# Windowed attention and channel mix on one core: every engine in the order of a list schedule, with k and q cast on chip

## The chip, the core and the metric

One NeuronCore of a Trainium2 chip runs the whole program. The metric is the device time of one execution in microseconds. The kernel before took 205.57 us (median of 3 runs, 205.5 to 205.82).

## The reference

Attention with a window of 128 positions and 4 sink positions, over 4 batches, 8 heads, 768 positions, head size 64; then an FFN over the 512 channels of all heads.

```python
scores = scale * q @ k.T                      # scale = 1/8
keep = is_sink | ((rel >= 0) & (rel < 128))   # rel = query position - key position; 4 sinks
a = softmax(where(keep, scores, -1e9))
x = (a @ v), heads side by side               # 4 x 768 x 512
xk = mu_k * x + (1 - mu_k) * x_prev           # x_prev: x of the position before
xr = mu_r * x + (1 - mu_r) * x_prev
out = sigmoid(xr @ w_r) * ((relu(xk @ w_k) ** 2) @ w_v)   # d_ff = 1024
```

## The kernel before

The work is cut into 12 units: `u = 3 b + T` is the 256 positions T of batch b. A unit with T = 0 has no positions before it, needs no sink scores and fewer values; there are 4 such units and 8 others.

**A unit's attention.** `prepare` (L164) transposes k and q on TensorE (L172, four 128x128 transposes a group, four groups a unit) into one bank, and ScalarE copies them out (L175). `sink_scores` (L198) and `scores` (L207) work on pairs of heads (c = 0 to 3): six matmuls (four where T = 0) into the one score tile `sc`, the exponential on ScalarE (L222) into `e`, the mask on VectorE (L228, or L231 where T = 0), then `values` (L234): matmuls of `e` with v (L255) and of the sinks (L244), and on VectorE a reciprocal (L259) and the product (L260) that gives `x`. GpSimd casts v to bf16 (L179).

**A unit's FFN.** `transposed` (L267) turns x (L275, copied by ScalarE at L279), `mix` (L281) makes xk and xr on VectorE (a difference td at L294, four steps each at L298). `ffn` (L302) has the keys (L311: four groups of eight 128x256 matmuls; relu on ScalarE L315, square on VectorE L316), the gate (L323, two groups of four 512-wide matmuls; tanh at L326) and the product (L331, four groups of four 512-wide matmuls; VectorE L336 joins gate and product), and SP stores the result (L339).

**What sets the order.** On TensorE a loop written by hand (L382 to L446): for each n (a unit and a pair of heads) a piece of the current unit's attention, a piece of the FFN of an earlier unit (`fill`), a quarter of the next unit's `prepare`. The order on SP up to unit 2's loads (L86 to L94) is fixed as well; on the other engines a scheduler sets it. Fillers on a tile of zeros (`idle`, L356) stand in TensorE's first part, 35 in all.

**Loads.** For units 0 to 2, k and q come as fp32 through SP's queue and are transposed as fp32. For the others, `load` (L65, L76) issues them from GpSimd's queue with bf16 destinations, so that the transfer casts them. v is always fp32 through SP. Each of k, q and v has three buffers. The weights come as fp32 through SP (L89, L91, L93); w_k and w_r are cast by GpSimd (L366, L369), and w_v is scaled and cast by VectorE (L372).

**PSUM.** Of eight banks two hold `sc`, two are `tps` (transposes, sink scores), one `o`, three `mm`.

Of the kernel before, what the change touches and what calls it, by code (L numbers as in the profile page):

```python
# [13 lines left out]
PSUM = bass.MemoryType.PSUM  # L14


@with_exitstack
def kernel(
# [28 lines left out]
    ld = ctx.enter_context(tc.tile_pool(name="ld", bufs=3))  # L47
    kt_pool = ctx.enter_context(tc.tile_pool(name="kt", bufs=3))
    e_pool = ctx.enter_context(tc.tile_pool(name="e", bufs=3))
    x_pool = ctx.enter_context(tc.tile_pool(name="x", bufs=2))  # L50
    kk_pool = ctx.enter_context(tc.tile_pool(name="kk", bufs=2))
    r_pool = ctx.enter_context(tc.tile_pool(name="r", bufs=3))
# [6 lines left out]
    raw = {}  # L59

    def dtype(u, name):

        return FP32 if u < 3 or name == "v" else BF16

    def load(u, names="kqv", halves=1):  # L65
        b, T = divmod(u, NT)
        for name in names:
            if (u, name) not in raw:
                raw[u, name] = ld.tile([128, 2, H, D], dtype(u, name), name=name + ("s" if dtype(u, name) == FP32 else "b"))
        n = H // halves  # L70
        for i in range(halves):
            for name in names:
                for g in range(2):
                    s0 = 256 * T + 128 * g
                    ahead = dtype(u, name) != FP32
                    ins = (nc.gpsimd if ahead else nc.sync).dma_start(  # L76
                        out=raw[u, name][:, g, n * i:n * i + n, :],
                        in_={"k": k, "q": q, "v": v}[name][
                            b, n * i:n * i + n, s0:s0 + 128, :].rearrange("h p d -> p h d"))
                    if ahead:  # L80
                        tc.keep_in_program_order(ins)

    wk32 = const.tile([128, NC, Dff], FP32, name="wk32")
    wr32 = const.tile([128, NC, Dm], FP32, name="wr32")
    wv32 = const.tile([128, NF, Dm], FP32, name="wv32")
    with tc.manual_schedule(engines={mybir.EngineType.SP}):  # L86
        load(0, "kq", 2)
        load(0, "v")
        nc.sync.dma_start(out=wk32, in_=moe_w_k.rearrange("(c p) f -> p c f", p=128))  # L89
        load(1, "kq")  # L90
        nc.sync.dma_start(out=wr32, in_=moe_w_r.rearrange("(c p) f -> p c f", p=128))  # L91
        load(1, "v")
        nc.sync.dma_start(out=wv32, in_=moe_w_v.rearrange("(c p) f -> p c f", p=128))  # L93
        load(2)  # L94


    warm = const.tile([128, 512], BF16, name="warm")
    nc.vector.memset(warm, 0.0)
    ident32 = const.tile([128, 128], FP32, name="ident32")
    make_identity(nc, ident32)  # L100
    ident = const.tile([128, 128], BF16, name="ident")
    nc.gpsimd.tensor_copy(out=ident, in_=ident32)


    mask = const.tile([128, 2, 2, 2, 128], BF16, name="mask")
    mask0 = const.tile([128, 2, 3, 128], BF16, name="mask0")
# [9 lines left out]
    nc.gpsimd.memset(mask0, 1.0)  # L116
    keep(mask0[:, :, 0, :], "D")
    keep(mask0[:, :, 1, :], "U")
    keep(mask0[:, :, 2, :], "D")
    nc.gpsimd.memset(mask0[0:NS, :, 0:2, :], 1.0)  # L120

    wk_sb = const.tile([128, NC, Dff], BF16, name="wk_sb")
    wr_sb = const.tile([128, NC, Dm], BF16, name="wr_sb")
    wv_h = const.tile([128, NF, Dm], BF16, name="wv_h")
    mu_k_sb = const.tile([128, NC], FP32, name="mu_k_sb")
    nc.scalar.dma_start(out=mu_k_sb, in_=moe_mu_k.rearrange("(c p) -> p c", p=128))
    mu_r_sb = const.tile([128, NC], FP32, name="mu_r_sb")
    nc.scalar.dma_start(out=mu_r_sb, in_=moe_mu_r.rearrange("(c p) -> p c", p=128))

    nc.gpsimd.memset(mask, 1.0)  # L130
    for a in range(2):
        keep(mask[:, a, :, 0, :], "U")
        keep(mask[:, a, :, 1, :], "D")

    v_bufs = [const.tile([128, 2, H, D + 1], BF16, name=f"v{i}") for i in range(3)]
    for t in v_bufs:
        nc.gpsimd.memset(t[:, :, :, D:D + 1], 1.0)

    xts = [const.tile([128, NC, S + 2], BF16, name=f"xt{i}") for i in range(2)]
    for t in xts:  # L140
        nc.gpsimd.memset(t[:, :, 0:2], 0.0)

    ksink = [const.tile([128, NP * 136], BF16, name=f"ksink{i}") for i in range(2)]
    vsink = [const.tile([128, H, D + 1], BF16, name=f"vsink{i}") for i in range(2)]
    for t in ksink + vsink:
        nc.gpsimd.memset(t, 0.0)
    hmask = const.tile([32, H, D + 1], BF16, name="hmask")
    nc.gpsimd.memset(hmask, 1.0)
    nc.gpsimd.affine_select(out=hmask, in_=hmask, compare_op=ALU.is_ge, fill=0.0, base=0,
                            pattern=[[-4, H], [0, D + 1]], channel_multiplier=1)  # L150
    nc.gpsimd.affine_select(out=hmask, in_=hmask, compare_op=ALU.is_ge, fill=0.0, base=3,
                            pattern=[[4, H], [0, D + 1]], channel_multiplier=-1)
    for t in vsink:
        nc.gpsimd.tensor_copy(out=t[0:32, :, D:D + 1], in_=hmask[:, :, D:D + 1])

    spread = const.tile([128, 128], BF16, name="spread")
    nc.gpsimd.memset(spread, 0.0)
    nc.gpsimd.tensor_copy(out=spread[0:NS, 0:4 * H].rearrange("p (h s) -> p h s", s=NS),
                          in_=ident[0:NS, 0:NS].unsqueeze(1).to_broadcast([NS, H, NS]))


    kqt = {}

    def prepare(u, name, half):  # L164
        if half == 0:
            kqt[u, name] = kt_pool.tile([128, NP, 2, 128], BF16, name=name + "t")
        src, dst = raw[u, name], kqt[u, name]
        ps = tr_ps.tile([128, 2, 2, 128], dtype(u, name), name="tps")
        for i in range(2):
            for g in range(2):  # L170
                c = 2 * half + i
                nc.tensor.transpose(out=ps[:, i, g, :],  # L172
                                    in_=src[:, g, 2 * c:2 * c + 2, :].rearrange("p a d -> p (a d)"),
                                    identity=ident32 if dtype(u, name) == FP32 else ident)
        nc.scalar.copy(out=dst[:, 2 * half:2 * half + 2, :, :], in_=ps)  # L175
# [126 lines left out]
    def ffn(u):  # L302
# [25 lines left out]
        for g in range(2):  # L328
            ps = mm_ps.tile([128, Dm], FP32, name="mm")
            for f in range(NF):  # L330
                nc.tensor.matmul(out=ps, lhsT=kk[:, f, 128 * g:128 * g + 128],  # L331
                                 rhs=wv_h[:, f, :], start=(f == 0), stop=(f == NF - 1))
                if f == NF // 2 - 1:
                    yield
# [149 lines left out]
```

## Time and profile before

| what | value |
|---|---|
| median of the runs | 205.57 us |
| the profiled execution | 205.31 us |
| its span | 203.6 us |
| mean granted TensorE clock | 0.966 |
| busy: TensorE, VectorE, ScalarE, GpSimd | 89%, 70%, 61%, 33% |
| transpose of k waiting for its load (kb) | 6.1 us, 4 times, the longest 2.9 |
| GpSimd's DMA issues for k and q | 31.9 us, 36 issues |

The span goes from the first to the last instruction; the profiled execution's own time is 1.71 us longer. Busy shares are of the whole span. L numbers are lines of the kernel before unless the text says otherwise. Names are those of the program (kb, qb: k and q as bf16; kt, qt: transposed; mm: an FFN bank).

### The profile page before, as it was taken

The page shows a single profiled execution, that of the slowest core. Times are in us where ns is not written, and L with a number is a line of the kernel's source. Part 1 is how long each engine was busy: PE and PEld are TensorE (multiplying, and loading weights), DVE is VectorE, ACT ScalarE, POOL GpSimd, SP SyncE. Part 2 cuts the span into 40 slices and gives each one's busy share as a digit, 9 for nine tenths or more (in the row PEclk, how much of TensorE's full clock was granted, in tenths as well). Part 3 has the DMA queues.
Part 4 walks back from the last instruction along what each step waited for, and adds up shares of the span by engine and source line. Part 5 has one row for each costly group of instructions (what it writes and reads, how often), then busy time and mean ns, then how long its engine had stood idle before and what let it go on. Part 6 is the DMA issues. An engine that isn't in the chain of part 4 may idle for free.

```text
span 203.6 us, 4309 instructions
## 1 busy us (share of the span) xinstructions
PE 180.9 (89%) x1681; PEld 115.9 (57%) x1704; DVE 142.5 (70%) x345; ACT 125.2 (61%) x201; POOL 68.0 (33%) x106
## 2 busy tenths in 40 slices
PE   7976869853998999999998999999999999999992
PEld 2633636531584665665855656666647567566650
DVE  0079486950776995986878959858969688698731
ACT  2443527541586586795875785967857868756340
POOL 8947160172149922002389420031890000000000
PEclk9999669996699999999999999999999999999999
DMA  6999999879969999205299992002996011020202
GB/s 117 230 392 212 281 292 279 164 106 166 245 118 127 201 217 67 104 2 131 78 103 181 234 104 106 0 3 106 80 107 125 3 56 48 3 103 3 101 2 103
DMA packets 81572, 25.97 MB, mean 128 GB/s; under 512 B 76432, under 2 KB 76432, under 8 KB 81552
## 3 DMA queue, kind: packets, MB, share of 16 engines
q1 hardware_dynamic: 43056, 20.98, 41.2%
q0 software_dynamic: 37440, 4.72, 36.3%
q8 instruction: 13, 0.21, 0.4%
q10 hardware_dynamic: 1056, 0.00, 0.3%
q14 instruction: 7, 0.06, 0.1%
HBM read 24.12 MB, written 6.29 MB: 149 GB/s over the span
## 4 chain that ended last, share of the span: by engine, by line
PE 37%; DVE 20%; SPq 17%; DMA 10%; ACT 8%; issue 5%; POOL 2%; DVEq 0%; ACTq 0%
SPq L76 13%; PE mm L311 12%; DMA kb<-in_k_dram 8%; PE mm L323 8%; PE mm L331 7%; DVE o_sb L336 5%; DVE xk L298 5%; ACT e L222 4%; ACT kt L175 3%; DVE xr L298 2%; SPq L93 2%; DMA vs<-in_v_dram 2%; PE tps L172 2%; PE o L255 2%; DVE e L228 2%
## 5 line engine op out<-in xcount | busy, mean ns | idle before, releaser
L311 PE MATMUL mm<-xk,wk_sb 128*128 128x256 bf16 x384 | 52.1, 277 | 3.2 <-DVE xk L298 3.1
L222 ACT ACTIVATE e<-sc 128x1024 bf16<-128x1024 f32 (+1 forms) x48 | 45.9, 956 | 10.9 <-PE sc L218 10.1
L331 PE MATMUL mm<-wv_h,kk 128*128 128x512 bf16 x182 | 47.7, 385 | 1.0 <-DVE wv_h L372 0.3
L228 DVE TENSOR_TENSOR e<-e,mask 128x1024 bf16<-128x1024 bf16 x32 | 22.1, 690 | 28.9 <-ACT e L222 28.9
L315 ACT ACTIVATE rl<-mm 128x512 bf16<-128x512 f32 x48 | 28.9, 603 | 20.8 <-PE mm L311 17.6
L311 PEld LDWEIGHTS <-wk_sb 128*128 128x128 bf16 x384 | 35.2, 99 | 10.5 <-issue 5.0
L179 POOL CAST v<-vs 128x512 bf16<-128x512 f32 x24 | 18.5, 788 | 56.4 <-PE o L255 30.8
L298 DVE SCALAR_TENSOR_TENSOR xk<-td,mu_k_sb,xt 128x256 bf16<-128x256 bf16 x48 | 26.1, 578 | 0.0
L331 PEld LDWEIGHTS <-kk 128*128 128x128 bf16 x192 | 16.7, 99 | 14.0 <-issue 1.3
L323 PE MATMUL mm<-wr_sb,xr 128*128 128x512 bf16 x84 | 22.1, 380 | 0.7 <-issue 0.2
L298 DVE SCALAR_TENSOR_TENSOR xr<-td,mu_r_sb,xt 128x256 bf16<-128x256 bf16 x48 | 22.4, 499 | 0.0
L316 DVE TENSOR_TENSOR kk<-rl 128x512 bf16<-128x512 bf16 x48 | 20.0, 417 | 3.1 <-ACT rl L315 3.1
L255 PE MATMUL o<-v,e 128*128 128x65 bf16 x352 | 20.6, 194 | 1.1 <-DVE e L231 1.0
L255 PEld LDWEIGHTS <-e 128*128 128x128 bf16 x352 | 17.7, 98 | 5.9 <-DVE e L231 1.8
L260 DVE TENSOR_TENSOR x<-o,rec 128x256 bf16<-128x256 f32 x48 | 20.1, 420 | 0.7
L231 DVE TENSOR_TENSOR e<-e,mask 128x768 bf16<-128x768 bf16 x16 | 10.3, 641 | 14.8 <-ACT e L222 14.7
L336 DVE SCALAR_TENSOR_TENSOR o_sb<-th,mm 128x512 f32<-128x512 f32 x24 | 16.3, 679 | 4.0 <-PE mm L331 4.0
L175 ACT COPY kt<-tps 128x512 bf16<-128x512 bf16 x18 | 10.5, 583 | 13.9 <-PE tps L172 13.9
L218 PE MATMUL sc<-qt,kt 64*128 64x128 bf16 (+1 forms) x256 | 18.5, 244 | 0.0
L175 ACT COPY qt<-tps 128x512 bf16<-128x512 bf16 x18 | 10.5, 583 | 9.5 <-PE tps L172 9.5
L218 PEld LDWEIGHTS <-kt 64*128 64x128 bf16 x256 | 8.7, 95 | 13.3 <-issue 10.9
L76 POOL DMA_DIRECT2D qb<-in_q_dram x18 | 16.0, 907 | 0.0
(56 smaller groups left out, 211.4 us busy)
## 6 DMA issues: line engine op xcount, KB each, us to landing
vs<-in_v_dram SPq DMA_DIRECT2D x24, 256.0 KB, 5.2
out_dram<-o_sb SPq DMA_DIRECT2D x24, 256.0 KB, 2.0
kb<-in_k_dram POOLq DMA_DIRECT2D x18, 128.0 KB, 5.0
qb<-in_q_dram POOLq DMA_DIRECT2D x18, 128.0 KB, 5.8
wk<-in_moe_w_k_dram SPq DMA_DIRECT2D x1, 2048.0 KB, 9.4
wv<-in_moe_w_v_dram SPq DMA_DIRECT2D x1, 2048.0 KB, 13.6
ks<-in_k_dram SPq DMA_DIRECT2D x4, 256.0 KB, 10.1
qs<-in_q_dram SPq DMA_DIRECT2D x4, 256.0 KB, 5.9
```

Source lines behind the costliest of these rows:

```text
L76: ins = (nc.gpsimd if ahead else nc.sync).dma_start(out=raw[u, name][:, g, n * i:n * i + n, :], in_={"k": k, "q": q, "v": v}[name][b, n * ...
L175: nc.scalar.copy(out=dst[:, 2 * half:2 * half + 2, :, :], in_=ps)
L218: nc.tensor.matmul(out=sc[:, a, o0:o1], lhsT=lhs[rows], rhs=rhs[rows], start=True, stop=True)
L222: nc.scalar.activation(out=e[:, :, lo:], in_=sc[:, :, lo:], func=AF.Exp, scale=scale)
L228: nc.vector.tensor_tensor(out=e, in0=e, in1=mask.rearrange("p a g k q -> p a (g k q)"), op=ALU.mult)
L255: nc.tensor.matmul(out=o[:, g, a, :], lhsT=e[:, a, e0:e0 + 128], rhs=rhs, start=(T == 0 and i == 0), stop=(i == len(blocks) - 1), skip_gro ...
L298: nc.vector.scalar_tensor_tensor(out=dst[:, c0 + i, :], in0=td[:, i, :], scalar=mu[:, c0 + i:c0 + i + 1], in1=prv[:, i, :], op0=ALU.mult, ...
L311: nc.tensor.matmul(out=ps[:, i, :], lhsT=wk_sb[:, c, 128 * f:128 * f + 128], rhs=xk[:, c, :], start=(c == 0), stop=(c == NC - 1), skip_gro ...
L315: nc.scalar.activation(out=rl, in_=ps, func=AF.Relu)
L323: nc.tensor.matmul(out=ps, lhsT=xr[:, c, 128 * g:128 * g + 128], rhs=wr_sb[:, c, :], start=(c == 0), stop=(c == NC - 1))
L331: nc.tensor.matmul(out=ps, lhsT=kk[:, f, 128 * g:128 * g + 128], rhs=wv_h[:, f, :], start=(f == 0), stop=(f == NF - 1))
L336: nc.vector.scalar_tensor_tensor(out=o_sb, in0=th[g], scalar=1.0, in1=ps, op0=ALU.add, op1=ALU.mult)
```

## The change

The loops that emitted the work are replaced. Each step of the work (a group of matmuls, a cast, a load) is now an entry with an engine, a cost in ns, a rank, what it reads and writes, which buffers it takes from a pool and which it holds. `Plan.schedule` simulates the engines with these costs and repeatedly picks the step that can start earliest, with the lower rank first where two could start at the same time. The steps are then emitted in that order under a manual schedule of all engines. Ranks grow by 10 a unit, in the order attention, mix, next unit's preparation, FFN of the unit before.

Beside the order, five things change. All k and q come as fp32 through SP. ScalarE casts each unit's k and VectorE its q, in two halves (512 columns each), so that all transposes are bf16. w_k and w_r are cast by VectorE, no longer by GpSimd. The six PSUM banks beside `sc` are one pool for all uses. Eight fillers remain of 35.

```diff
+FFN_AFTER = 10
+CAST = {"k": "ACT", "q": "DVE"}
...
+                for i in some:
+                    o = ops[i]
+                    t = max(now, at[i])
+                    if o["port"]:
+                        t = max(t, port.get("DVE" if engine == "POOL" else "POOL", 0.0))
...
+                    if pick is None or (t, o["rank"], i) < (pick[0], ops[pick[1]]["rank"], pick[1]):
+                        pick = (t, i)
...
-    sc_ps = ctx.enter_context(tc.tile_pool(name="sc_ps", bufs=1, space=PSUM))
-    tr_ps = ctx.enter_context(tc.tile_pool(name="tr_ps", bufs=2, space=PSUM))
-    o_ps = ctx.enter_context(tc.tile_pool(name="o_ps", bufs=1, space=PSUM))
-    mm_ps = ctx.enter_context(tc.tile_pool(name="mm_ps", bufs=3, space=PSUM))
+    pool("sc", 1, [128, 2, 512], FP32, psum)
+    pool("bank", 6, [128, 512], FP32, psum)
+    for name in ("ks", "qs", "vs"):
+        pool(name, 3, [128, 2, H, D], FP32)
+    pool("kb", 2, [128, 2, H, D], BF16)
+    pool("qb", 2, [128, 2, H, D], BF16)
...
+                P.op("SP", rows * 0.9 + 60.0, emit, rank, service=rows * 1.19 + 60.0,
...
+    for i in range(4):
+        sl = slice(256 * i, 256 * i + 256)
+        P.op("DVE", dve(1024, 0.52), lambda sl=sl: nc.vector.tensor_copy(
+            out=wk_sb[:, :, sl], in_=wk32[:, :, sl]), 2 + i, reads=["wk32"], writes=[("wk", i)],
+            port=True)
...
+            by = CAST[name]
+            if by:
+                copy = {"ACT": nc.scalar.copy, "DVE": nc.vector.tensor_copy,
+                        "POOL": nc.gpsimd.tensor_copy}[by]
+                cost = {"ACT": act(512), "DVE": dve(512, 0.52), "POOL": gps(512)}[by]
+                P.op(by, cost, lambda copy=copy, raw=raw, rk=rk, hs=hs: copy(
+                    out=buf[rk][:, :, hs, :], in_=buf[raw][:, :, hs, :]), rank + half,
...
+    idle(8, -200, ("idle", 0))
+    prepare(0, 0)
+    for u in range(U):
+        attend(u, 10 * u + 4)
+        if u + 1 < U:
+            prepare(u + 1, 10 * u + 11)
+        mix(u, 10 * u + 8)
+        if u > 0:
+            ffn(u - 1, 10 * u + FFN_AFTER)
+    ffn(U - 1, 10 * U + FFN_AFTER)
+    with tc.manual_schedule():
+        P.run()
```

Three places show how the instructions move.

VectorE, unit 0's attention, before (rec and x normalize a pair of heads, td and xk are the mix; the last masks stand between them):

```order
L231 TENSOR_TENSOR e<-e,mask_138 128x2x384
L259 RECIPROCAL rec<-o 128x4
L260 TENSOR_TENSOR x<-o,rec 128x2x128
L231 TENSOR_TENSOR e<-e,mask_138 128x2x384
L192 TENSOR_TENSOR vsink_168<-tps,hmask 32x8x64
L294 TENSOR_TENSOR td<-xt_162 128x512
L259 RECIPROCAL rec<-o 128x4
L298 SCALAR_TENSOR_TENSOR xk<-td,mu_k_sb,xt_162 128x256 x2
L260 TENSOR_TENSOR x<-o,rec 128x2x128
```

And now (wk_119 is the loaded w_k, e_88 and e_89 the last two pairs of heads, bank_62 to bank_64 the values of the first three):

```order
L493 TENSOR_TENSOR e_88<-e_88,mask_128 128x2x384
L493 TENSOR_TENSOR e_89<-e_89,mask_128 128x2x384
L436 TENSOR_TENSOR vsink_133<-bank_67,hmask 32x8x64
L354 CAST wk_sb<-wk_119 128x4x256 x4
L530 RECIPROCAL rec_92<-bank_62 128x4
L530 RECIPROCAL rec_93<-bank_63 128x4
L530 RECIPROCAL rec_94<-bank_64 128x4
L533 TENSOR_TENSOR x_95<-bank_62,rec_92 128x2x128
L533 TENSOR_TENSOR x_95<-bank_63,rec_93 128x2x128
```

The four casts of w_k, which GpSimd had, now stand ahead of all normalization of unit 0.

ScalarE, whose copies follow TensorE's groups, around the first keys of unit 1's FFN (rl), before (the first COPY of kt is unit 3's k, the es and the first e belong to unit 2):

```order
L205 ACTIVATE es<-tps 128x256
L222 ACTIVATE e<-sc 128x1024
L175 COPY kt<-tps 128x512
L222 ACTIVATE e<-sc 128x1024
L279 COPY xt_162<-tps 128x2x256
L175 COPY qt<-tps 128x512
L222 ACTIVATE e<-sc 128x1024
L315 ACTIVATE rl<-mm 128x512 x2
L175 COPY kt<-tps 128x512
```

And now (kt_83 and qt_84 are unit 2's, rl_107 is of unit 1's first keys, kb_78<-ks_68 is the cast of unit 3's k):

```order
L406 COPY kt_83<-bank_63 128x512
L562 COPY xt_129<-bank_65 128x2x256
L406 COPY qt_84<-bank_62 128x512
L484 ACTIVATE e_86<-sc_61 128x1024
L406 COPY qt_84<-bank_63 128x512
L607 ACTIVATE rl_107<-bank_67 128x512
L484 ACTIVATE e_87<-sc_61 128x1024
L457 ACTIVATE es_91<-bank_62 128x256
L382 CAST kb_78<-ks_68 128x2x256
```

The first keys of unit 1 stood behind unit 3's first transposed k and three exponentials of unit 2; now they stand behind one exponential of unit 2 and ahead of all of unit 3.

The loads of unit 3, before on GpSimd (v_157 is unit 1's v, v_158 unit 2's, v_156 unit 3's; kb and qb are unit 3's k and q):

```order
L179 CAST v_157<-vs 128x8x64 x2
L179 CAST v_158<-vs 128x8x64 x2
L76 DMA kb<-in_k_dram 128x8x64 x2
L76 DMA qb<-in_q_dram 128x8x64 x2
L179 CAST v_156<-vs 128x8x64 x2
```

And now on SP (wv_121 is the loaded w_v, ks_70, qs_73 and vs_76 are unit 2's, ks_68, qs_71 and vs_74 unit 3's):

```order
L248 DMA wv_121<-in_moe_w_v_dram 128x8x512
L237 DMA ks_70<-in_k_dram 128x8x64 x2
L237 DMA qs_73<-in_q_dram 128x8x64 x2
L237 DMA vs_76<-in_v_dram 128x8x64 x2
L237 DMA ks_68<-in_k_dram 128x8x64 x2
L237 DMA qs_71<-in_q_dram 128x8x64 x2
L237 DMA vs_74<-in_v_dram 128x8x64 x2
```

Unit 3's k and q stood behind GpSimd's cast of unit 2's v; now they stand directly behind the load of that v.

More of the change, by code (lines that the diff above doesn't have):

```diff
@@ L54, with pool @@
[L54 to L65 removed]
+    psum = ctx.enter_context(tc.tile_pool(name="psum", bufs=1, space=PSUM))
+    P = Plan()
+    def pool(name, n, shape, dtype, where=const):
+        P.pool(name, [where.tile(shape, dtype, name=f"{name}{i}") for i in range(n)])
@@ L71, in load @@
[L71 to L94, printed above, removed]
@@ new lines, with const_op @@
+    for u in range(2, U):
+        load(u, "kqv", -92 if u == 2 else 10 * u - 18)
+    for i, src in enumerate((moe_mu_k, moe_mu_r)):
+        P.op("ACT", 600.0, lambda i=i, src=src: nc.scalar.dma_start(
+            out=mu[i], in_=src.rearrange("(c p) -> p c", p=128)), -100, writes=[("mu", i)],
+            service=300.0)
+    def const_op(engine, cost, emit, writes=(), reads=(), rank=-50):
+        P.op(engine, cost, emit, rank, writes=writes, reads=reads, port=engine == "POOL")
+    warm = tile1([128, 512], BF16, "warm")
@@ L126 @@
[L126 to L159, printed above, removed]
@@ L162 @@
[L162 to L175, printed above, removed]
```

718 lines of the change are left out of this document (460 added, 258 removed).

## The prediction

> **What bounds the kernel now.** I read the page first, then the windows, the chain of waits and TensorE's timeline. The span, TensorE's busy time and the chain's shares by line:
>
> ```profile
> span 203.6 us, 4309 instructions
> ...
> PE 180.9 (89%) x1681; PEld 115.9 (57%) x1704; DVE 142.5 (70%) x345; ACT 125.2 (61%) x201; POOL 68.0 (33%) x106
> ...
> SPq L76 13%; PE mm L311 12%; DMA kb<-in_k_dram 8%; PE mm L323 8%; PE mm L331 7%; DVE o_sb L336 5%; DVE xk L298 5%; ACT e L222 4%; ACT kt L175 3%; DVE xr L298 2%; SPq L93 2%; DMA vs<-in_v_dram 2%; PE tps L172 2%; PE o L255 2%; DVE e L228 2%
> ```
>
> TensorE looks full, but 21% of the chain is the loads of L76 on SP and the k loads (kb). So there are two regimes. In the middle, a window of 60 us from steady running (columns: TensorE, weight loads, VectorE, ScalarE, GpSimd, granted clock, DMA share):
>
> ```profile
> 80.00:140.00 60.00, 58.06 (x606) 38.67 (x613) 48.38 (x123) 43.91 (x72) 17.23 (x22) 1.00 0.66 94
> ```
>
> TensorE is 97% busy at full clock, VectorE 81%, ScalarE 73%. At the beginning it is otherwise. The chain of waits in order of time (start, length, what):
>
> ```profile
> 35.74 4.55 DMA vs<-in_v_dram
> 40.34 0.85 POOL v L179
> 41.19 0.95 POOL kb L76
> 42.14 7.34 DMA kb<-in_k_dram
> 49.53 0.50 PE tps L172 x3
> ```
>
> Unit 3's k is loaded through GpSimd's queue, behind GpSimd's cast of unit 2's v; that v came at 40.3 us. TensorE, whose order puts unit 3's first transposes ahead of the rest of unit 2, then waits until 49.5. The two marks from which I work are the start of unit 1's and of unit 11's FFN in TensorE's timeline:
>
> ```profile
> 54.35 0.39 PE L311 MATMUL mm<-xk,wk_sb 128*128 128x256 bf16 x2
> ...
> 190.86 3.66 PE L311 MATMUL mm<-xk,wk_sb 128*128 128x256 bf16 x32
> ```
>
> Between them lie ten steps of (190.86 - 54.35) / 10 = 13.65 us, and behind the second mark 203.6 - 190.86 = 12.74 us. The execution took 205.31 us, 1.71 over its span, and is 0.26 under the median of 205.57. Before = 54.35 + 10 x 13.65 + 12.74 + 1.71 + 0.26 = 205.57; I predict each term.
>
> **How much of a step is TensorE's own work.** Its timeline in a dense stretch; I read distances from start to start, since the lengths overlap:
>
> ```profile
> 118.87 0.35 PE L255 MATMUL o<-v,e 128*128 128x65 bf16 x6
> 119.05 1.03 PE L331 MATMUL mm<-wv_h,kk 128*128 128x512 bf16 x4
> 119.91 0.39 PE L172 MATMUL tps<-ident,kb 128*128 128x128 bf16 x4
> 120.23 0.39 PE L218 MATMUL sc<-qt,kt 64*128 64x256 bf16 x6
> 120.56 0.40 PE L275 MATMUL tps<-ident,x 128*128 128x128 bf16 x4
> 120.79 1.03 PE L331 MATMUL mm<-wv_h,kk 128*128 128x512 bf16 x4
> ...
> 122.88 0.39 PE L172 MATMUL tps<-ident,qb 128*128 128x128 bf16 x4
> 123.10 1.03 PE L331 MATMUL mm<-wv_h,kk 128*128 128x512 bf16 x4
> ...
> 128.63 0.22 PE L244 MATMUL o<-vsink,es 128*128 128x130 bf16 x1
> ...
> 128.99 1.04 PE L311 MATMUL mm<-xk,wk_sb 128*128 128x256 bf16 x8
> 129.86 0.39 PE L172 MATMUL tps<-ident,qb 128*128 128x128 bf16 x4
> ```
>
> Four 512-wide matmuls take 0.86 us, eight 256-wide 0.87, a group of k transposes 0.32 and of q 0.22, six scores 0.33, x transposes 0.23, one pair of heads through the values 0.36 (0.18 where there is no sink). A unit with sinks is therefore 2 x 0.32 + 2 x 0.22 (k and q) + 0.44 (sink scores, half of eight 256-wide) + 4 x 0.33 + 4 x 0.36 + 2 x 0.23 + 4 x 0.87 (keys) + 2 x 0.86 (gate) + 4 x 0.86 (product) = 13.4 us; a unit that starts a sequence has no sink scores and cheaper values, 12.2. The attentions within the ten steps are seven of the first and three of the second kind: 130.4 us, or 13.04 a step. So only 0.6 of the 13.65 us can be won in a step, while the first mark at 54.35 has much room.
>
> **The change at the first mark.** Up to unit 2 the loads on SP stand in the same order, so weights and v land when they did. Rows of before, from the timeline and from the page's list of DMA issues:
>
> ```profile
> 16.32 4.75 POOL L366 CAST wk_sb<-wk 128x1024 bf16<-128x1024 f32 x4 [3.90 <-DMA wk<-in_moe_w_k_dram]
> ...
> 17.85 2.32 DVE L298 SCALAR_TENSOR_TENSOR xk<-td,mu_k_sb,xt 128x256 bf16<-128x256 bf16 x2
> ...
> 20.09 4.70 SPq L93 DMA_DIRECT2D wv<-in_moe_w_v_dram  x1
> ```
>
> ```profile
> wv<-in_moe_w_v_dram SPq DMA_DIRECT2D x1, 2048.0 KB, 13.6
> ```
>
> w_k is there at 16.3 and w_v at 20.1 + 13.6 = 33.7. The weight casts go from GpSimd to VectorE; the nearest row is VectorE's scaling of w_v, 0.62 for each of four, and two other VectorE rows price what follows (the second gives shortest, median and longest):
>
> ```profile
> 35.78 2.49 DVE L372 TENSOR_SCALAR wv_h<-wv 128x1024 bf16<-128x1024 f32 x4
> ```
>
> ```profile
> L260 DVE TENSOR_TENSOR x<-o,rec 128x256 bf16<-128x256 f32 x48 | 20.1, 420 | 0.7
> ```
>
> ```profile
> L298 DVE SCALAR_TENSOR_TENSOR xk<-td,mu_k_sb,xt x48: 469/477/2110, 17.9 to 190.4; 128x256 bf16<-128x256 bf16 x48
> ```
>
> The four w_k casts stand ahead of unit 0's normalization on VectorE. This is an added wait: queued behind it are the reciprocals and x of unit 0, and TensorE, ScalarE and VectorE wait for these in turn. 16.3 + 4 x 0.62 = 18.8; four x with their reciprocals, at most 0.6 each, 21.2; transposes and copy about 1.0; two td, a q cast and four xk about 3, so unit 0's keys begin near 25. Before, they stand at 24.9 with a stall to 27.6, so this wait replaces one of its size and I give it nothing. Up to 35 TensorE then has keys (3.5), gate (1.7) and unit 1's attention (3.7), 8.9 us: it must wait for w_v. At 33.7 VectorE casts two quarters (35.0) and TensorE begins unit 0's product. All four are done at 36.2, the rest of unit 1's x at 38.0, transposes and copy at 39.0, then td, one q cast, td and four xk, 2.6: unit 1's keys start at **41.6** in place of 54.35. Nothing of unit 3 stands ahead of them, and its loads follow v of unit 2 directly on SP. The earliest is 39 (VectorE hides the x work); the latest 46, if unit 2's k and q come 4 us after w_v, as they are on SP.
>
> Filler matmuls go from 35 to 8. Their cover was the clock. After the wait that ended at 49.5 the window shows it:
>
> ```profile
> 49.00:56.00 7.00, 6.16 (x49) 3.77 (x50) 3.58 (x8) 3.53 (x5) 1.23 (x2) 0.62 1.47 222
> ```
>
> 0.62 over 7 us is 2.7 us lost. The same at unit 0's keys would turn 8.9 us of work into 11.6 from 25 on, 36.6. That is 1.6 us past 35.0, but VectorE is then still casting w_v, to 36.2, and its x work sets the mark; I take 0 and keep 0 to 1.6. The Trainium skill, "TensorE: Matmul & The Clock Gate", Part 1, speaks against dropping fillers: after about 3.4 us of idleness the array runs at half clock until about 3.4 us of sustained work have passed. By it the loss would be an estimated 1.7 us, which leaves the sum as it is; this trace's loss is larger, 2.7, and the measurement decides.
>
> **The change in a step.** GpSimd loses 36 DMA issues; k and q come as fp32 through SP, between its v loads and its stores. From the list of waits:
>
> ```profile
> SPq L339 <- DVE rec L259: 73.8, 10, 11.6
> ```
>
> SP spends 73.8 us waiting in stores, so 36 more issues cost nothing there; a load behind a store could come late, but the loads stand two units ahead. Added are two k casts on ScalarE and two q casts on VectorE a unit. No row shows them; the nearest for ScalarE:
>
> ```profile
> L175 ACT CAST kt<-tps x6: 581/585/586, 6.6 to 40.7; 128x512 bf16<-128x512 f32 x6
> ```
>
> So 1.17 us a step on ScalarE (10.0 + 1.2 of 13.65). On VectorE half of a 0.62 us cast is 0.31, and an isolated one costs at most the 0.42 of L260's row: 0.6 to 0.8 on 11.0. Both stay under TensorE's 13.04. What can go is the rest of 0.6 a step. The fp32 transposes of units 0 to 2 lie before the first mark and are hidden behind loads. From both ends, 13.04 (nothing waits) and 13.9 (0.25 worse for fuller engines), I take **13.4**, nearer the middle since each TensorE group now stands where its operands are planned ready. The slow xk of 17.85 us, 2.32 for two, ran while GpSimd cast w_k; with GpSimd's casts of weights and its issues gone, VectorE's xk should stay at its median 0.48. The Trainium skill, "SBUF — State Buffer", section "SBUF: two separate sides", calls the port pair of VectorE and GpSimd a lock on which the loser blocks wholly. By it the 24 q casts also hold back GpSimd's v casts; the row above agrees with blocking, and an estimated step would lie between 13.04 and 13.4.
>
> Sum: 41.6 + 134.0 + 12.74 + 1.71 + 0.26 = **190.3 us**.
>
> **The rivals.**
> VectorE paces the step, still faster: it is fullest (11.0 + 0.8 of 13.65), and six banks now serve transposes, values and FFN alike, so a late VectorE holds TensorE. Against it: 11.8 is still only 88% of a 13.4 us step. At 14.3 a step the time is 199.3. Chance 0.12.
> The early stall survives in another form: cold clock to the first mark, or unit 2's k and q late, with 50 to 54 there: 198.7 to 202.7. Against it: the loads are no later than before. Chance 0.05.
> Slower than before: VectorE keeps all its present idleness, 13.65 - 11.0 = 2.65 us a step, because its static order meets the exponentials too early, and adds the casts. That is 14.5, or 201.3. It decides from a step of 14.93, where it loses 3.1 us to waits; at 15.2 the time is 208.3. For it: one score tile in both kernels, four masks a unit. Against it: FFN work stands between the masks. Chance 0.07.
> That the change does nothing is excluded by the order, where casts and loads have moved.
>
> **How the numbers follow.** The forecast has 0.76, its own range 186 (39 and 13.2) to 199 (46 and 13.8). The faster rivals fill 199 to 203, where most of VectorE's lies at the lower end. From 185 to 200 holds eight in ten. About 0.2% is what a measurement of this kernel can tell from no change. Faster: 0.76 + 0.12 + 0.04 = 0.92; same 0.01; slower 0.07.
>
> **What would show it.** Right: unit 1's keys near 41.6 us in TensorE's timeline, no wait for kb of several us, ten steps of about 13.4, w_v's casts just before unit 0's product, VectorE under 90% in the middle. Wrong: the first mark past 47; a step over 13.9 with TensorE waiting for VectorE or ScalarE; or low clock after 30 us.

## The result

The changed kernel takes **191.27 us** (median of 4 runs, 190.66 to 192.09) where the kernel before takes 205.69 on the same chip: a ratio of 0.929, 95% interval 0.924 to 0.934. The forecast was 190.3, within 185 to 200. Some executions of any of these kernels are slow ones; ratios and intervals use the fast ones alone, medians all.

The profiled execution took 191.44 us, 13.87 less than the one before. Its page, in the order of the lines shown of before:

```profile
span 189.7 us, 4373 instructions
...
PE 171.4 (90%) x1676; PEld 111.1 (59%) x1676; DVE 155.9 (82%) x375; ACT 133.4 (70%) x225; POOL 31.9 (17%) x65
...
PE bank L598 18%; PE bank L636 18%; PE bank L621 8%; PE sc L476 6%; DMA ks<-in_k_dram 5%; PE bank L517 4%; DVE xk L577 4%; PE bank L395 4%; SPq L237 3%; DVE kk L611 3%; DVE e L493 3%; DVE xr L577 2%; DVE qb L382 2%; PE bank L449 2%; PE bank L556 2%
```

The 21% of the chain that were loads (L76, k, q and v on SP, and kb) are 8% now (ks and L237), and FFN matmuls (L598 keys, L636 product, L621 gate) stand in their place. TensorE's busy time fell by 9.5 us (180.9 to 171.4), its idle time by 4.4 (22.7 to 18.3). The idle time of before is overstated: 23 of its matmuls have no record (1681 against 1704 weight loads), and some of what shows as idle is theirs.

The two marks in TensorE's timeline, the start of unit 1's and of unit 11's keys:

```profile
41.67 0.81 PE L598 MATMUL bank<-xk,wk_sb 128*128 128x256 bf16 x4
...
177.18 3.66 PE L598 MATMUL bank<-xk,wk_sb 128*128 128x256 bf16 x32
```

So the sum is 41.67 + 10 x 13.55 + 12.52 + 1.74 = 191.4. Of the 13.87 us gained, 12.7 lie ahead of the first mark, 1.0 in the ten steps, 0.2 behind. What TensorE did up to that mark, before (windows, then its filler group) and after:

```profile
0.00:54.35 54.35, 41.03 (x303) 24.22 (x306) 28.94 (x56) 23.92 (x37) 26.93 (x53) 0.87 1.08 224
```

```profile
L360 PE MATMUL mm<-warm 128*128 128x512 bf16 x35 | 11.1, 453 | 1.3 <-DVE warm L98 1.3
```

```profile
0.00:41.67 41.67, 29.22 (x239) 17.53 (x239) 27.92 (x60) 23.62 (x37) 16.04 (x41) 0.75 1.04 252
```

```profile
L660 PE MATMUL bank<-warm 128*128 128x512 bf16 x8 | 3.6, 631 | 1.3 <-DVE warm L272 1.3
```

Fillers stand where TensorE would wait. Idle time and fillers together were 54.35 - 41.03 + 11.1 = 24.4 us and are 41.67 - 29.22 + 3.6 = 16.1, so by this count 8.3 of the 12.7 us are waiting that went; 7.5 of these are fillers. The other 4.4 are work that is shorter (bf16 in place of fp32 transposes) or no longer stands ahead of that mark. This split hangs on the clock, 0.87 before and 0.75 here: work at a lower clock takes longer and fills waits. With 27 fillers put back (the last experiment) the clock up to the mark is 0.92 and the mark 41.32. Idle time and fillers are then 41.32 - 32.22 + 10.6 = 19.7 us, and of the 13.0 us by which that mark moved only 4.7 are waiting that went:

```profile
0.00:41.32 41.32, 32.22 (x266) 17.99 (x267) 26.65 (x60) 23.69 (x37) 16.06 (x41) 0.92 1.02 250
```

```profile
L371 PE MATMUL bank<-warm 128*128 128x512 bf16 x21 | 5.4, 379 | 0.0
L666 PE MATMUL bank<-warm 128*128 128x512 bf16 x8 | 3.4, 606 | 1.3 <-DVE warm L272 1.3
...
L371 PE MATMUL sc<-warm 128*128 128x512 bf16 x6 | 1.8, 377 | 2.0 <-ACT e L490 2.0
```

The middle, in the columns of before's row (TensorE, weight loads, VectorE, ScalarE, GpSimd, clock, DMA share, GB/s):

```profile
80.00:140.00 60.00, 58.37 (x596) 37.67 (x594) 55.21 (x134) 46.31 (x79) 9.30 (x14) 1.00 0.63 149
```

TensorE is as full as before (58.37 against 58.06), VectorE is at 92% in place of 81%. All of TensorE's waits after 60 us:

```profile
PE bank L517 <- DVE e L493: 1.5, 2, 1.2
```

### The profile page after: what moved, and what is told of

Same layout as the page of the kernel before. It is cut to its first block, busy times and chain, and to the rows that moved or that the text cites. A ratio compares the mean times of both kernels' runs of the same rounds, so it can differ in the third digit from the quotient of the medians.

```text
span 189.7 us, 4373 instructions
## 1 busy us (share of the span) xinstructions
PE 171.4 (90%) x1676; PEld 111.1 (59%) x1676; DVE 155.9 (82%) x375; ACT 133.4 (70%) x225; POOL 31.9 (17%) x65
## 4 chain that ended last, share of the span: by engine, by line
PE 64%; DVE 20%; DMA 5%; ACT 4%; SPq 4%; issue 2%; ACTq 0%; DVEq 0%
PE bank L598 18%; PE bank L636 18%; PE bank L621 8%; PE sc L476 6%; DMA ks<-in_k_dram 5%; PE bank L517 4%; DVE xk L577 4%; PE bank L395 4%; SPq L237 3%; DVE kk L611 3%; DVE e L493 3%; DVE xr L577 2%; DVE qb L382 2%; PE bank L449 2%; PE bank L556 2%
## 5 line engine op out<-in xcount | busy, mean ns | idle before, releaser
L598 PE MATMUL bank<-xk,wk_sb 128*128 128x256 bf16 x384 | 54.7, 279 | 0.1
L636 PE MATMUL bank<-wv_h,kk 128*128 128x512 bf16 x192 | 47.1, 380 | 0.0
L598 PEld LDWEIGHTS <-wk_sb 128*128 128x128 bf16 x384 | 35.2, 100 | 7.0 <-issue 1.1
L493 DVE TENSOR_TENSOR e<-e,mask 128x1024 bf16<-128x1024 bf16 (+1 forms) x48 | 31.1, 653 | 8.5 <-ACT e L484 8.4
L607 ACT ACTIVATE rl<-bank 128x512 bf16<-128x512 f32 x48 | 29.2, 630 | 7.4 <-PE bank L598 6.6
L413 POOL CAST vb<-vs 128x512 bf16<-128x512 f32 x24 | 17.4, 741 | 74.4 <-DMA vs<-in_v_dram 45.7
L636 PEld LDWEIGHTS <-kk 128*128 128x128 bf16 x192 | 17.1, 98 | 19.1 <-issue 1.1
L621 PE MATMUL bank<-wr_sb,xr 128*128 128x512 bf16 x96 | 24.5, 380 | 0.0
L577 DVE SCALAR_TENSOR_TENSOR xk<-td,mu,xt 128x256 bf16<-128x256 bf16 x48 | 23.2, 507 | 0.5
L577 DVE SCALAR_TENSOR_TENSOR xr<-td,mu,xt 128x256 bf16<-128x256 bf16 x48 | 22.4, 490 | 0.0
L645 DVE SCALAR_TENSOR_TENSOR ob<-th,bank 128x512 f32<-128x512 f32 x24 | 16.3, 681 | 6.7 <-PE bank L636 6.7
L517 PE MATMUL bank<-vb,e 128*128 128x65 bf16 x352 | 20.1, 197 | 1.6 <-DVE e L493 1.5
L533 DVE TENSOR_TENSOR x<-bank,rec 128x256 bf16<-128x256 f32 x48 | 19.6, 419 | 0.7
## 6 DMA issues: line engine op xcount, KB each, us to landing
wv<-in_moe_w_v_dram SPq DMA_DIRECT2D x1, 2048.0 KB, 13.8
```

Source lines behind the costliest of these rows:

```text
L493: nc.vector.tensor_tensor(out=buf[ek][:, :, lo:], in0=buf[ek][:, :, lo:], in1=m, op=ALU.mult)
L517: nc.tensor.matmul(out=o[:, g, a, :], lhsT=e[:, a, e0:e0 + 128], rhs=rhs, start=(T == 0 and i == 0), stop=(i == len(blocks) - 1), skip_gro ...
L533: P.op("DVE", dve(256), lambda ok=ok, rk=rk, c=c: nc.vector.tensor_tensor(out=buf["x", u][:, :, 128 * c:128 * c + 128].rearrange("p g (a d ...
L577: nc.vector.scalar_tensor_tensor(out=buf[key][:, c0 + i, :], in0=buf[tk][:, i, :], scalar=mu[w][:, c0 + i:c0 + i + 1], in1=xt[:, c0 + i, t ...
L598: nc.tensor.matmul(out=ps[:, i, :], lhsT=wk_sb[:, c, 128 * f:128 * f + 128], rhs=xk[:, c, :], start=(c == 0), stop=(c == NC - 1), skip_gro ...
L607: P.op("ACT", act(512), lambda psk=psk, rk=rk: nc.scalar.activation(out=buf[rk], in_=buf[psk].rearrange("p (i t) -> p i t", i=2), func=AF. ...
```

## The experiments

Each was timed against the kernel before on its own chip. Before's median was between 204.91 and 205.53 there, so ratios are compared. Marks and steps are those of each profiled execution.

| kernel | median, us | ratio to before, interval | first mark | step |
|---|---|---|---|---|
| before | 205.57 | 1 | 54.35 | 13.65 |
| before, unit 3's k and q by SP | 204.28 | 0.997, 0.992 to 1.002 | 52.16 | 13.78 |
| changed, second measurement | 191.64 | 0.929, 0.924 to 0.934 | 39.99 | 13.56 |
| changed, casting loads from 12 us on | 200.99 | 0.984, 0.977 to 0.991 | 49.68 | 13.77 |
| changed, casting loads behind unit 2's v | 190.90 | 0.926, 0.921 to 0.930 | 42.65 | 13.46 |
| changed, no casts, fp32 transposes | 196.93 | 0.961, 0.955 to 0.967 | 42.52 | 13.88 |
| changed, order undone at one place | 194.19 | 0.942, 0.938 to 0.946 | 50.81 | 12.94 |
| changed, plan with half costs | 215.73 | 1.048, 1.043 to 1.053 | 47.02 | 15.52 |
| changed, q cast by GpSimd | 190.07 | 0.929, 0.922 to 0.936 | 41.03 | 13.39 |
| changed, q cast by ScalarE | 191.01 | 0.932, 0.928 to 0.937 | 43.15 | 13.39 |
| changed, w_v cast by GpSimd | 194.92 | 0.953, 0.949 to 0.957 | 43.35 | 13.75 |
| changed, q and w_v cast by GpSimd | 200.87 | 0.981, 0.975 to 0.987 | 48.67 | 13.79 |
| changed, fillers kept | 191.87 | 0.941, 0.935 to 0.946 | 41.32 | 13.59 |

The changed kernel measured again sets the scale: its first mark was 41.67 in one profiled execution and 39.99 in the other, and its runs went from 189.88 to 192.55. Less than 1% between two versions is not told apart here.

> The changed kernel itself, so that variants are compared on one chip: 190.5 to 192.2 by every theory.

### Is it unit 3's load alone?

The kernel before, with unit 3's k and q loaded as fp32 through SP, so that they no longer stand behind GpSimd's cast of unit 2's v:

```diff
-        return FP32 if u < 3 or name == "v" else BF16
+        return FP32 if u < 4 or name == "v" else BF16
```

> The kernel before with one line changed: k and q of unit 3 too come as fp32 through SP and are transposed as fp32. Theory A, the early gain is the load of unit 3 that no longer stands behind GpSimd's cast of unit 2's v: the wait of 5.4 us before 49.5 and the 2.7 us of low clock behind it go, unit 1's keys start near 46.3 in place of 54.35, and the time is about 197.5 (196 to 199). Theory B, the early gain is the order, with unit 1's keys ahead of unit 3: the wait only changes its releaser, unit 1's keys stay past 50, and the time is 202 to 205.6.

The time is the same (interval 0.992 to 1.002). TensorE's timeline before, unit 3's first transposes, then that of this kernel with unit 1's keys:

```profile
46.78 0.23 PE L172 MATMUL tps<-ident,kb 128*128 128x128 bf16 x1 [2.89 <-DMA kb<-in_k_dram]
49.53 0.50 PE L172 MATMUL tps<-ident,kb 128*128 128x128 bf16 x3 [2.52 <-DMA kb<-in_k_dram]
```

```profile
46.30 0.30 PE L172 MATMUL tps<-ident,ks 128*128 128x128 f32 x1 [1.94 <-DMA ks<-in_k_dram]
47.40 0.55 PE L172 MATMUL tps<-ident,ks 128*128 128x128 f32 x3 [0.80 <-DMA ks<-in_k_dram]
...
52.16 0.50 PE L311 MATMUL mm<-xk,wk_sb 128*128 128x256 bf16 x3
```

The rest of unit 3's k comes 2.1 us sooner (47.40 for 49.53), and TensorE's two waits for it are 2.7 us in place of 5.4. Mark and time are those of theory B, but theory A had taken the wait as gone, and it is only halved: TensorE's order by hand still stands at it while the FFN of unit 1 is held behind. Halving the wait that the chain named gives 2.2 us at the mark and nothing at the end that can be told. What removing it whole would give no run shows.

### Are the SP loads and the casts what gains?

The changed kernel with k and q of units 3 to 11 loaded by GpSimd with the cast in the transfer, as before, and no casts on ScalarE and VectorE for them. First with nothing to hold these loads back, then with each of them reading the cast of unit 2's v:

```diff
+                    P.op("POOL", 950.0, lambda key=(name + "b", u), src=src, g=g, s0=s0:
+                         nc.gpsimd.dma_start(
+                             out=buf[key][:, g, :, :],
...
+                         reads=[("vb", 2, 1)], writes=[(name, u, g, hp) for hp in range(2)])
...
-            if by:
+            if u > 2:
+                raw = rk
+            elif by:
```

(The first of the two is without the `reads` entry. The second also emits these loads later, each unit's just ahead of its `prepare`.)

> The changed kernel with the load path undone: k and q of units 3 to 11 come as bf16 by casting DMAs on GpSimd's queue, so 36 DMA issues return there and 36 casts leave ScalarE and VectorE; the schedule places them anew. If the load path and the casts make the gain, unit 1's keys start past 46 and the time is 196 or more. If the order makes it, unit 1's keys start at 41 to 44 and, with 0.7 us a unit less on VectorE, the time is 187 to 192.

> The changed kernel with the load path undone as before: k and q of units 3 to 11 by casting DMAs on GpSimd's queue, those of unit 3 only behind the cast of unit 2's v, as in the kernel before; the order around unit 1's keys stays that of the changed kernel. If the order makes the early gain, unit 1's keys start at 41 to 42.5 although unit 3's k comes at 49 or so, and with 24 casts less on VectorE the time is 188 to 191. If the load path is needed for it, unit 1's keys start past 46 and the time is 196 or more.

The first comes out as expected of a gain by the load path (mark 49.68, 200.99 us), the second as expected of one by the order (42.65, 190.90 us). Held back, the old loads are as fast as the new ones with their casts: 0.926 against 0.929, intervals that overlap. From unit 3 on the casts on chip and the loads through SP give nothing by themselves. Let go at once, the twelve loads run beside the weights. GpSimd's timeline of that kernel shows the first of them, SP's the issue of w_v, VectorE's the casts that follow its landing:

```profile
12.74 2.05 POOL L240 DMA_DIRECT2D kl<-in_k_dram  x2
```

```profile
25.63 3.69 SPq L260 DMA_DIRECT2D wv<-in_moe_w_v_dram  x1
```

```profile
41.80 2.50 DVE L375 TENSOR_SCALAR wv_h<-wv 128x1024 bf16<-128x1024 f32 x4 [3.46 <-DMA wv<-in_moe_w_v_dram]
```

In the changed kernel w_v is issued at 20.11 and its casts start at 34.22. So w_v comes 7.6 us later here, of which 5.5 are SP's queue, held up ahead of it, and the rest a slower transfer, and most of the 10 us that this kernel loses is lost there. That the loads keep behind the weights is thus a condition of the gain, though not its source.

The other way about, no casts at all and every transpose of k and q in fp32:

```diff
-CAST = {"k": "ACT", "q": "DVE"}
+CAST = {"k": None, "q": None}
```

> The changed kernel without the casts of k and q: all transposes of k and q are fp32, in a list schedule of their own. In the kernel before, an fp32 group of four transposes is 0.60 long and a bf16 group 0.39, and their spacing 0.58 against 0.22 to 0.32: some 0.3 us more for each of four groups a unit. Theory, TensorE's own work sets the step once VectorE and ScalarE have room: 13.04 + 1.2 = 14.2 to 14.6 a step, and 198 to 202 us. Rival, TensorE's work is covered by waits for VectorE: VectorE loses 1.1 us a unit and ScalarE 1.3, their waits go, and the step stays at 13.5 to 13.9: 191 to 195 us.

196.93 us, 3.9% below the kernel before, though that one has bf16 transposes from unit 3 on and this one has none. The middle, and the spacing of such a group (0.44 from its start to the next, 0.32 and 0.22 for bf16 groups):

```profile
80.00:140.00 60.00, 60.00 (x585) 40.44 (x584) 49.96 (x118) 43.96 (x71) 8.29 (x14) 1.00 0.63 145
```

```profile
88.00 0.60 PE L395 MATMUL bank<-ident,ks 128*128 128x128 f32 x4
88.44 0.22 PE L505 MATMUL bank<-vsink,es 128*128 128x130 bf16 x1
```

TensorE has no idle time left. By this spacing a unit's own work would be 13.04 + 4 x 0.44 - 1.08 = 13.72, and a step takes 13.88. The time lies between the two expectations and the step within the rival's; yet TensorE's own work sets it, as the theory had it, with a surcharge of 0.17 a group in place of 0.3 (before, too, an fp32 group was 0.44 from the next, 38.76 to 39.20; the expectation's 0.58 was too long). So the change gains 3.9% even with transposes that are dearer than before's; the 3% between this kernel and the changed one are about what bf16 transposes are worth, which from unit 3 on the kernel before had too.

### Is it the order?

In the changed kernel, unit 1's second x transposes made to wait for unit 3's first transposed k, as in the order by hand, with unit 3 prepared a unit sooner:

```diff
-                 reads=["ident", ("x", u, c0), ("x", u, c0 + 1)], writes=[psk])
+                 reads=["ident", ("x", u, c0), ("x", u, c0 + 1)] +
+                 ([("kt", 3, 0)] if (u, half) == (1, 1) else []), writes=[psk])
...
-        if u + 1 < U:
-            prepare(u + 1, 10 * u + 11)
+        for w in {1: (2, 3), 2: ()}.get(u, (u + 1,)):
+            if w < U:
+                prepare(w, 10 * w + 1)
```

> The changed kernel with one added dependence: the second x transposes of unit 1 wait for unit 3's first transposed k, as they stood behind it in the kernel before; the schedule places the rest anew, loads and casts stay. If this order is what cost the time before, these transposes start near 46.5 in place of 38.3, unit 1's keys near 50 in place of 41.7, and the time is 197 to 202. If the order there is worth nothing, the time stays within 1 us of the changed kernel's.

The rows of its two marks:

```profile
50.81 2.50 PE L599 MATMUL bank<-xk,wk_sb 128*128 128x256 bf16 x20
...
180.18 3.66 PE L599 MATMUL bank<-xk,wk_sb 128*128 128x256 bf16 x32
```

The mark is 9.1 us later, the profiled execution only 3.0 (194.46), and the step falls to 12.94: 6 us of the later mark are work of units 2 and 3 that TensorE did meanwhile and need not do later. The first mark is where the order would put it (near 50), but the time, 194.19, lies below the 197 to 202 that were expected with it. One place of the order costs 1.4% (0.942 against 0.929), and a mark is not yet a loss.

Then the same list schedule with costs that are wrong:

```diff
+        if engine in ("DVE", "ACT"):
+            cost = 0.5 * cost
```

> The changed kernel with the plan's costs of VectorE's and ScalarE's steps halved, so that the order is made for engines twice as fast. If the early gain needs only an order that keeps later units out of the way, unit 1's keys still start at 41 to 43, the step grows from 13.55 to 13.7 to 14.2, and the time is 193 to 198. If the gain needs the measured costs, the time is 200 or more; if the costs do not matter, it is within 1 us of the changed kernel's.

It is 4.8% slower than the kernel before the change: the gain needs the measured costs. Its middle and its largest waits of TensorE after 60 us:

```profile
80.00:140.00 60.00, 52.42 (x536) 34.99 (x543) 49.00 (x122) 43.86 (x75) 6.38 (x10) 1.00 0.57 129
```

```profile
PE bank L558 <- DVE x L535: 5.6, 7, 1.5
PE bank L519 <- DVE e L495: 5.5, 11, 1.3
PE sc L478 <- ACT e L486: 2.0, 4, 0.8
```

No engine is fuller than in the changed kernel; all are emptier. The same instructions on the same engines, put where VectorE and ScalarE should have been done but are not, give a step of 15.52. That is the mechanism of the prediction's slower rival, and the costs in the plan are what kept it away.

What the change brought beside the order can be bounded at the first mark. Unit 0's product, the first work that needs w_v, starts at 36.52 before and at 34.94 now:

```profile
36.52 1.20 PE L331 MATMUL mm<-wv_h,kk 128*128 128x512 bf16 x4 [0.31 <-DVE wv_h L372]
```

```profile
34.94 2.05 PE L636 MATMUL bank<-wv_h,kk 128*128 128x512 bf16 x8
```

So what acts ahead of it, w_k and w_r cast by VectorE among it, is worth some 1.6 of the 12.7 us there; 11.1 lie behind it, where the order differs. (Unit 2's fp32 transposes stand there too, before; but the kernel without casts has fp32 transposes as well, and its mark is at 42.52.) The six PSUM banks as one pool no run changes alone, so their share stays open.

### What holds a step at 13.55?

The casts of q on GpSimd, and on ScalarE:

```diff
-CAST = {"k": "ACT", "q": "DVE"}
+CAST = {"k": "ACT", "q": "POOL"}
```

> The changed kernel with the q casts on GpSimd. If VectorE, 92% busy in the middle, sets the 0.5 us that a step has over TensorE's own 13.04, the step falls from 13.55 to 13.2 or 13.3 and the time to 187.5 to 189. If GpSimd's casts hold up VectorE as much as they relieve it, or TensorE's own work is all, the time stays within 190.5 to 193.

> The changed kernel with the casts of q on ScalarE as well as those of k. If VectorE's fullness (55.21 of 60 us) is what keeps a step at 13.55 over TensorE's own 13.04, VectorE falls by two casts a unit and the step falls to about 13.4, as it did with these casts on GpSimd: 190 us. Rival: the step is held by the exchange between TensorE and the two engines whichever of them is fuller; ScalarE goes from 46.3 to about 52 of 60 us (two casts of 0.667 a unit) and the step stays at 13.5 to 13.9: 191 to 195 us.

Both have a step of 13.39. The middle with GpSimd's casts, then with ScalarE's:

```profile
80.00:140.00 60.00, 59.73 (x623) 38.60 (x621) 53.59 (x124) 46.57 (x81) 14.29 (x22) 1.00 0.61 145
```

```profile
80.00:140.00 60.00, 59.02 (x606) 37.42 (x600) 52.94 (x126) 52.27 (x92) 8.02 (x13) 1.00 0.65 150
```

With VectorE at 53.6 or 52.9 in place of 55.2, 0.16 us a step go, whichever engine takes the casts. For GpSimd step and time lie between the two expectations; for ScalarE the step is that of the theory and the time that of the rival. On ScalarE the gain is given back at the first mark (43.15): there w_v's casts start at 35.18, 1.0 later than in the changed kernel, and TensorE waits for them:

```profile
35.93 2.06 PE L636 MATMUL bank<-wv_h,kk 128*128 128x512 bf16 x8 [1.10 <-DVE wv_h L363]
```

Neither median can be told from the changed kernel's.

The 0.16 is not yet the price of the casts on VectorE, since each kernel has a list schedule of its own. The middle with w_v's cast on GpSimd, with both w_v's and q's there (next section), and with the casting loads behind v:

```profile
80.00:140.00 60.00, 59.08 (x605) 38.52 (x603) 54.99 (x135) 48.64 (x85) 7.94 (x14) 1.00 0.63 148
```

```profile
80.00:140.00 60.00, 58.89 (x635) 39.70 (x635) 52.27 (x123) 47.70 (x83) 11.52 (x19) 1.00 0.61 144
```

```profile
80.00:140.00 60.00, 58.29 (x597) 37.59 (x603) 55.02 (x129) 43.57 (x72) 20.15 (x28) 1.00 0.82 103
```

Between the first two the q casts leave VectorE and the step goes from 13.75 to 13.79; in the third VectorE has no q casts from unit 3 on, is as full as ever, and the step is 13.46. So that VectorE's fullness holds the step at 13.55 is not shown.

### What sets the first mark?

The scaling and cast of w_v on GpSimd:

```diff
-        P.op("DVE", dve(1024, 0.52), lambda i=i: nc.vector.tensor_scalar(
+        P.op("POOL", gps(1024), lambda i=i: nc.gpsimd.tensor_scalar(
```

> The changed kernel with the scaling and cast of w_v on GpSimd in place of VectorE. Theory C, VectorE's chain sets the start of unit 1's keys: the four casts, 2.47 us at 34.22, stand ahead of the rest of unit 1's x, so without them the keys start up to 2.4 us sooner, 39.3 in place of 41.67, and the time falls by 1.0 to 2.4 us, to 189 to 190.3. Rival: TensorE's own work sets it, since TensorE is busy 11.03 of the 12 us up to the mark; then at most 0.97 us can go and the product of unit 0 waits for GpSimd, which needs about 1.5 us for each of four casts by its v casts (0.741 for half as many columns): the time stays at 191 to 192.5.

GpSimd's row, and TensorE's products that wait for it:

```profile
34.42 11.17 POOL L363 TENSOR_SCALAR wv_h<-wv 128x1024 bf16<-128x1024 f32 x4 [6.51 <-DMA wv<-in_moe_w_v_dram]
```

```profile
37.25 1.01 PE L636 MATMUL bank<-wv_h,kk 128*128 128x512 bf16 x2 [1.92 <-POOL wv_h L363]
...
39.99 1.01 PE L636 MATMUL bank<-wv_h,kk 128*128 128x512 bf16 x2 [1.73 <-POOL wv_h L363]
```

2.8 us a cast, where 1.5 was expected: the product of unit 0, which stands ahead of unit 1's keys on TensorE, became the later path, the mark went to 43.35 and the time past both expectations. So VectorE's chain was not tested by itself. In the changed kernel TensorE has 0.97 us idle in the 12 us up to its mark, and the last xk of unit 1 ends near 42.2 on VectorE; the two paths end within half a microsecond of each other, and which one is last the runs leave open.

Both moves together, q and w_v on GpSimd:

> The changed kernel with the casts of q and of w_v both on GpSimd. If both relieve VectorE where it is the last to come, the gains add: first mark 39 to 40, step 13.4, 188 to 189.5 us. If either place is set by TensorE, the time is within 1 us of the changed kernel's, 190.3 to 192.

200.87 us, later than either and past both expectations: its w_v casts take 11.28 us, and unit 0's last products wait 2.43 for them. The gains expected at two places of the order did not add.

What moves the mark between executions is when w_v's casts start. In the second execution of the changed kernel:

```profile
32.51 2.50 DVE L363 TENSOR_SCALAR wv_h<-wv 128x1024 bf16<-128x1024 f32 x4 [0.25 <-DMA wv<-in_moe_w_v_dram]
```

```profile
39.99 0.75 PE L598 MATMUL bank<-xk,wk_sb 128*128 128x256 bf16 x4
```

The casts start at 32.51 there and at 34.22 in the first, 33.87 with the fillers of the next section, 35.17 with the casting loads behind v; the mark comes 7.48, 7.45, 7.45 and 7.48 us later. So from the start of these casts to the mark the chain has one length in all four, and the 1.7 us between the changed kernel's two marks lie ahead of it.

### Fillers

Twenty-seven fillers put back into the gaps of the first 20 us:

```diff
+                fillers(buf[psk], 3 if u == 0 else 9 if (u, name, half) == (1, "k", 0) else 0)
...
+                fillers(sc[:, 0, :], 2 if u == 0 and c else 0)
```

> The changed kernel with 27 fillers put back into the gaps of TensorE's first 20 us, the order of all else unchanged. Theory: the low clock from 10 to 29 us is covered by the wait for w_v, so the clock there rises, unit 1's keys stay at 41.7 within 0.4 and the time stays within 0.4 of the changed kernel's. Rival: the cold start costs the 1.6 to 2.7 us that the prediction kept at zero, unit 1's keys start at 39 to 40 and the time is 188.5 to 189.7.

The windows of the changed kernel, then of this one:

```profile
10.00:20.00 10.00, 4.72 (x48) 3.08 (x48) 6.47 (x15) 4.82 (x8) 3.81 (x9) 0.50 1.14 306
20.00:30.00 10.00, 8.65 (x62) 5.74 (x60) 8.89 (x20) 6.79 (x11) 1.67 (x2) 0.54 0.97 286
```

```profile
10.00:20.00 10.00, 7.43 (x66) 3.42 (x66) 6.51 (x15) 4.71 (x7) 3.98 (x9) 1.00 1.16 314
20.00:30.00 10.00, 7.96 (x63) 5.36 (x64) 9.05 (x20) 6.52 (x11) 1.53 (x2) 0.66 0.96 291
```

The clock is full from 10 to 20 us, little higher in the ten after, and the first mark is where it was (41.32), the last too (177.17). Nothing is gained (0.941, the changed kernel 0.929). In the changed kernel w_v lands at 33.9 (issued at 20.11, 13.8 to landing) and its casts start at 34.22, so the low clock ahead of them can have cost the mark 0.3 us at most.

## Why the prediction was right

| term | forecast | measured |
|---|---|---|
| first mark | 41.6 | 41.67 |
| ten steps | 134.0 | 135.5 |
| behind the last mark | 12.74 | 12.52 |
| execution over span | 1.71 | 1.74 |
| median over profiled | 0.26 | -0.17 |
| sum | 190.3 | 191.27 |

**The first mark.** Its steps stand in VectorE's and TensorE's timelines almost where they were put:

```profile
16.55 2.48 DVE L354 CAST wk_sb<-wk 128x1024 bf16<-128x1024 f32 x4
...
34.22 2.47 DVE L363 TENSOR_SCALAR wv_h<-wv 128x1024 bf16<-128x1024 f32 x4
```

```profile
34.94 2.05 PE L636 MATMUL bank<-wv_h,kk 128*128 128x512 bf16 x8
...
38.34 0.38 PE L556 MATMUL bank<-ident,x 128*128 128x128 bf16 x4
```

w_k cast from 16.55 (16.3), w_v from 34.22 (33.7), unit 0's product at 34.94 (35.0), the last x transposes at 38.34 and their copy some 0.6 later (39.0). Unit 0's keys began at 23.7, not 25, which the wait for w_v hid. The second execution had its mark at 39.99, so a hit within 0.1 is partly luck; 39 to 46 was the honest statement. What was right in kind is the chain, w_v's casts and then VectorE's x work, which took 7.45 us where 33.7 to 41.6, 7.9, was put.

**The step.** 13.55 for 13.4. VectorE got more than was added to it: from 60 to 180 us it is busy 107.27 of 120 us, 12.1 a step, where 11.0 + 0.8 was forecast; a q cast there takes 0.47 rather than 0.31 to 0.42. "VectorE under 90% in the middle" failed, with 92%. What that costs stays open: two kernels that take the q casts off it step in 13.39, a third, with w_v's cast on GpSimd too, in 13.79. The first rival, VectorE paces the step, did not come with its 14.3, and for the last 0.2 us it is neither shown nor excluded. TensorE's own work is also a little more than the 13.04 of spacings: with TensorE busy 59.7 of 60 us a step still takes 13.39.

**What the prediction had not seen.** It named two things for the early gain, that nothing of unit 3 stands ahead of unit 1's keys and that unit 3's loads no longer queue behind GpSimd's cast, and did not part them. The load was real, but halving its wait alone gave nothing (0.997), and with the old loads the changed kernel is as fast (0.926). What gains is the order: work which has its operands stands ahead of work that has not. And it took the whole 12.7 us by which the first mark moves as gained time. That came out, since the steps did not grow, but it was not argued: with the order undone at one place a mark 9.1 us later costs only 3.0.

**The other rivals.** The early stall did not survive: TensorE's waits for k, in bf16 now, are 4.4 us in all. The slower one did not come to pass, yet the plan with half costs shows that it lay one wrong table away. The clock term of 0 to 1.6 was 0.3 at most. And 0.2% was too fine for what a measurement can tell: the kernel before ranges from 202.04 to 207.06 on one chip.

## What to carry to other kernels

The wait that the chain names is where an in-order queue stands, and not always what it costs: undo that wait alone before crediting it. A list schedule is worth what its costs are worth, for the same scheduler gave 7% less or 5% more time with right and with halved costs. Where the work before a mark changes, count idle time and fillers up to it, since the mark's own shift also holds work that only moved, and compare such counts at one clock. A step that gets shorter when one thing moves to another engine is not yet that thing's price where the whole schedule is made anew.

## What the runs showed of the hardware

**The granted clock** was 0.50 and 0.54 between 10 and 30 us of the changed kernel, although TensorE was busy 8.65 us of the second ten; 27 fillers raised it to 1.00 and 0.66. The Trainium skill, "TensorE: Matmul & The Clock Gate", Part 1, has the array at half rate until about 3.4 us of sustained work; the trace agrees in kind only. TensorE's waits in the second ten (0.7 us each) end at 23.20, and the clock is 0.50 until 29 and 0.86 from 29 to 30, so some 6 us of unbroken work passed; in the second execution they end at 22.69 and the clock is 0.63 from 24 to 26 and 1.00 from 26 on, 3.3 us at most. The time to full clock is not one number here.

**GpSimd's TENSOR_SCALAR** on 1024 columns took 2.8 us a piece in two kernels (11.17 and 11.28 for four), where GpSimd's CAST of 1024 columns took 1.2 in the kernel before (4.75 for four). Whether the operation or VectorE beside it makes the difference no run tells.

**VectorE's first cast of q** took 2.23 us at 6.05, in a stretch in which GpSimd was busy 9.06 of 10 us; with GpSimd idle at 21.44 such a cast takes 0.42:

```profile
6.05 2.23 DVE L382 CAST qb<-qs 128x512 bf16<-128x512 f32 x1 [4.86 <-DMA qs<-in_q_dram]
```

The Trainium skill, "SBUF — State Buffer", section "SBUF: two separate sides", says that one of the two engines holds a port pair for a whole instruction and the other blocks. The 1.8 us lost here are longer than any one of GpSimd's instructions beside it (0.7 us at most), so if it is that lock, VectorE lost it more than once. In the second execution the same cast took 0.43:

```profile
5.81 0.43 DVE L382 CAST qb<-qs 128x512 bf16<-128x512 f32 x1 [4.61 <-DMA qs<-in_q_dram]
```

GpSimd's instruction of that moment, in the first and in the second execution:

```profile
5.87 0.68 POOL L334 TENSOR_SCALAR_AFFINE_SELECT hmask<-hmask 32x520 bf16<-32x520 bf16 x1
```

```profile
5.85 0.92 POOL L334 TENSOR_SCALAR_AFFINE_SELECT hmask<-hmask 32x520 bf16<-32x520 bf16 x1
```

Where GpSimd began first, by 0.18 us, VectorE's cast was long; where VectorE began first, by 0.04, GpSimd's instruction was (0.92 for 0.68; spans on GpSimd are rough). No run tries this cast without GpSimd beside it.
